# The order of the steps in an attention and mixer kernel, written anew by a search: loads, constants and the first pairs in another sequence

## The chip, the cores and the metric

The kernel runs on 1 core of one Trainium2 chip. The metric is the device time of one execution in microseconds. Of the kernel before there are three runs: 692.95 us is their median, 691.92 and 696.07 the ends.

The engines are named as the profile has them: PE is TensorE (matmuls; PEld its weight loads), DVE VectorE, ACT ScalarE, POOL GpSimd, and SP is SyncE, which issues every transfer here.

## What is computed

An attention over 4 batches, 8 heads, 576 positions and 64 values per head, then two mixers over all positions. Its core, cut:

```python
# attention: q, k, v are (4, 8, 576, 64); factor 4
q_d, k_d, v_d = mean of 4 neighbours along the sequence       # 144 positions
out_up = repeat(softmax(scale * q_d @ k_d.T) @ v_d, 4)        # pooled part
scores = where(abs(i - j) < 4, scale * q @ k.T, -1e6)         # local part
attn = out_up + softmax(scores) @ v

# first mixer, x is (4, 576, 512)
h = relu(x.T @ w_tok1) @ w_tok2;  u = x + h.T
x = u + relu(u @ w_ch1) @ w_ch2

# second mixer
theta = x @ w_theta
y = w_tok_r @ (x * cos(theta)) + w_tok_i @ (x * sin(theta))
u = x + y;  out = u + relu(u @ w_ch)
```

The weights arrive as 64-bit floats; the kernel turns them into pairs of 32-bit parts (high and low) itself, and the products of the mixers are three matmuls each (high by high, high by low, low by high).

## The kernel before

The attention is worked in pairs: pair n is two heads of one batch (16 pairs), and two pairs are a quad Q (8 quads). Every part of the program is a Python generator that issues some instructions and yields; a step is one advance of one generator. The steps have letters:

- I: the constants. First advance: the transfer `fixed<-consts` (L288); second: memsets on POOL (L290, L292); third: ACT's cast of the identity `id16` (L294).
- P: loads the queries and keys of a pair, `qk_b_p` (L324, 582 KB, four buffers). W: loads the values of the local part, `vw` (L333, four transfers). V: loads the values of the pooled part, `vd` (L342), and sums them on POOL (L344, L347, L350).
- K: pools the queries and keys of a pair on DVE (L367, L368, out `qkd`).
- F: the pooled attention of a quad: scores `sd` on PE (L380, L389), their maximum `mxd` on DVE (L398, L406), the exponential `pd` on ACT (L409, L414, L419), its transposition `pdt` on PE (L423, L428), a copy `pts` on ACT (L431, L432), the product `od` on PE (L439 to L446), the division `ods` on DVE (L450 to L453), a store of it to memory (L456, L457) and later a read back, repeated, as `xu` (L462, L465).
- L: the local attention of a pair: warm matmuls on zeros that nobody reads (L279; 24, 12, 12 and 12 for the first four pairs), the mask's matmul (L476), scores `s` (L479), `mx` and `pbuf` on DVE (L491, L492), the exponential on ACT (L499), `pt` on PE (L504), copies on ACT (L507, L508), the product `o` (L514), the division into `x` on DVE (L523 to L528).
- A adds `xu` to `x` (L541). T, E and U are the first mixer's token products (`t`, L136 to L138 and L563, L564; hidden L586, L589; out L599, L602).
- G and X convert weights: a transfer `raw` (L162), two ACT instructions (L172, L173), three on DVE (L175, L177, L185), one on POOL (L189), one on ACT (L191), the low part on DVE (L193). G0 to G6 are the token weights, X the channel weights and those of the second mixer.
- C, H, O: the first part of the channel product, from `uh` and `ul`, the split of `ut` (L627); B, M, N its second part, whose last weights are `c22` to `c25` (L645, L646, L648). R and Z switch memory over and load the second mixer's input.

The scores `s`, `sd`, the transpositions `pdt`, `pt` and the product `o` share one pool of PSUM with two buffers, taken in turn in the order of the program. `qk` has four buffers, `vw` two. All transfers are issued by SP in the order of the steps; one that must wait for its buffer holds up those behind it.

The steps stand in a table, `ORDER` (L30 to L69), a string of 1110 names: `F0` advances the pooled attention of quad 0 by one step, `L0*2` the local attention of pair 0 by two. The kernel runs through it, and within an engine the instructions stay in the order in which they are issued:

```python
    with tc.manual_schedule(engines={act.engine, dve.engine, pool.engine, pe.engine, nc.sync.engine}):
        for e in ORDER:
            name, _, times = e.partition("*")
            for _ in range(int(times or 1)):
                next(gens[name], None)
```

Behind the table comes the rest of the second mixer (z, y, out), the same code in both kernels.

Of the kernel before, what the change touches and what calls it, by code (L numbers as in the profile page):

```python
# [35 lines left out]
X0 U0.0 F3 L4 U0.0 V4 K9 F2 F3 X0 L6 L4 L6 T1 F4 U0.1 X0 F3 T1 L5 U0.1 X0 T1 U0.1 F4 X7 X4 V4 F3 T1 X7 F4 W6 L5 X7
E1.1 F4 E1.0 E1.1 L8 V4 L8 X7 E1.0 X1 A4 F4 T1 P10 A5 T1 X2 T2 L8 T1 U1.0*2 T2 T1 U1.0 X1 F3 L7 X7 L7 T2 X1 T2 X4 X5
K10 X1 L8 L6 U1.1*2 L7 T2 E2.0 U1.1 W7 X4 L7 V4 X1 L7 F4 W9 L7 L6 X4 E2.1 E2.0 C0 E2.1 T2 X1 L8 K11 X5 L7 T2 X5 L8
W8 L9*2 L7 X5 P13 T2 P12 L9 L10 C0 A6 F5 X4 C0 U2.0 L10 U2.0 X5 U2.0 C0 X3 F5 X6 F4 F5 C0 A7 F4 L10 T3 X4 F5 L9 V5
T3 H0.1 L8 U2.1 F5 T2 H0.1 H0.0 K12 T3 L9 U2.1 X5 C0 L9 U2.1 K13 F4 X6*2 L10 T3 X3 W13 H0.0 X6 H0.2 F6 E3.0*2 V5 P14  # L40
T3 F6 V5 H0.2 F6 C0 V6 V5 L8 X3 E3.1 L9 H0.3 F5 E3.1 X3 W10 L9 F6 X3 F5 L10 V6 A9 T3 F5 T3 V6 U3.0 L10 K14 T3 V6
U3.0 X6 U3.0 T3 H0.3 X3 X6 L11*2 C0 L11 P15 U3.1*2 A8 F6 U3.1 C0 F5 T4 L11 L12 L10 O0.1 K15 C0 C1 W11 L10 O0.0 C0
T4*2 F7 O0.3 O0.2 L12 C1 O0.3 T4 L12 F7 L12 T4 C1 L11 E4.1 F6 L11 F7 L11 F6 C1 A10 W12 E4.0 L11 F6 F7 E4.0 A11 F7
L12 E4.1 C1 H1.0 T5 C2 F6 L13*2 H1.1 L12 H1.1 T4 T5 T4 U4.0 L13 C1 U4.0 H1.0 U4.0 L13 V7 T4 H1.2 T5 L13 L15 L13 T4
U4.1 L12 U4.1 L15 L12 W15 V7 C1 H1.2 A12 V7 U4.1 T5 H1.3 V7 H1.3 L13 E5.0 C1 L13 F7 C1 F7 E5.0 F7 L15 L14*2 A13 L15
C1 O1.0 L14 F7 O1.1 L14 T5 W14 C1 E5.1 C2 E5.1 T6 L14 L15 L14 T5 T6 T5 U5.0 C2 T5 U5.0 L15 U5.0 T5 O1.2 T6 O1.3*2
L15 L14 T6 U5.1 L14 U5.1*2 L15 T6 E6.0 A14 A15 C2 E6.1 C3 E6.0 T7 E6.1 T6 T7 H2.0 T6 U6.0 H2.0 T7*2 U6.0*2 C3 T6*2
T7 U6.1*2 E7.0 U6.1 C2 E7.1*2 E7.0 T7 H2.1*2 T7 U7.0 T7 U7.0*2 T7 C2*2 H2.2 U7.1 H2.2 U7.1 C3 U7.1 R0 X8 X17 H2.3
X11 H2.3 C2 X19 C2*2 X8 O2.1 X8 C2 O2.2 X8 O2.0 X11 C3 O2.3*2 X21 C3 H3.0 X19 H3.0 X19 X8 C3 X17 X8 X17 C4 H3.1 C3
H3.2*2 X17 H3.1 X19 X20 H3.3 X21 H3.3 C3 X11 X9 C3 C4 O3.0 X21 X17 X19 C3 C4 X21 C3 O3.2 X11 X21 X13 C4 O3.3 O3.1  # L50
X21 O3.3 X12 X17 X9 C4 X9 X20 X19 C4 X9 H4.0 X13 H4.0 X20 C5 C4 X15 H4.2 H4.1 X9 H4.1 X20 H4.2 H4.3 B2 X16 H4.3 C4
X9 X13 C4 C5 X13 X20 C4 O4.1 X12 X10 C5 X13 C4 O4.2 X12 B2 C5 O4.0 X12 X11 X13 C5 O4.3 H5.0 X20 X16 O4.3 X23 B2 C5
H5.1 X10 H5.0 X10 C5 H5.2 X12 X11 X10 H5.1 B2 H5.3 X14 X10 H5.3 J0 H5.2 X16 C5 M2.4 X23 X10 X16 X23 X15 C5 X18 C5
O5.1 X23 X22 B2 O5.2 O5.0 X12 X15 X14 C5 X23 X14 X16 M2.5 B2 O5.3 X14 X16 O5.3 R1 B2 X15 X40 X23 X18 X30 M2.6 B2 X18
M2.5 X18 B2 M2.8 X22 M2.8 X35 X22 M2.7 B2 X15 X14 M2.4 X22 M2.6 M2.9 X18 M2.7 B2 X15 X22 X33 X14 X40 X18 X40 X30 B0
X22 M2.10 X40 M2.11 M2.9 M2.11 M2.10 B2 X40 X36 X30 X35 B2 X35 X30 B0 X33 B0 X35 X24 B2 X33 X35 X38 X30 X40 X33 B0
X30 X28 B0 X38*2 X36 B0 X36 X38 X33 B2 X35 M0.4 X36 X39 X28 M0.4 X28 X29 X38 B0 X38 X28 B0 M0.7 X27 M0.5 X36 M0.5
M0.6 M0.7 X28 X36 B0 X39 M0.6 X39 M0.8 B0 X29 X33 X39 X28 M0.9 B0 M0.10 X27 M0.8 M0.9 M0.10 M0.11 B1 X27 X24 X37
X39*2 M0.11 B0 X24 B0 X24 B1 X27 X34 B1 X27 X25 B0 X24 N0.0 X27 X29 X34 N0.0 X29 B0 X34 X25 X31 X24 B1 N0.3*2 X25
N0.3 B1 M1.4 N0.1 X25 M1.4 N0.2 B1 X34 N0.3 M1.5 X37*2 B1 N0.2 X37 N0.2 B1 M1.7 X25 M1.7 X37 X32 M1.5 X26 X29 N0.0  # L60
B1 M1.6 X29 M1.6 X37 N0.1 B1 M1.9 N0.1 X31 M1.9 X31 M1.8 B1 X34 X32 M1.8 X31 X25 M1.11 B5 M1.10 J1 X26 M1.10 M1.11
B1 X26 X32 X26 B1 B5 X32 X26 B5 X32 B1 N1.0 N1.1*2 N1.0 N1.1 B1 B5 N1.3 X26 N1.2 N1.3 B5 X34 N1.3*2 B5 M5.5 N1.0
M5.4 B5 M5.6*2 M5.5 N1.2 B5 M5.4 N1.2 J2 B5*2 M5.9 M5.7 X31 M5.7 M5.8 M5.9 B5 M5.8 M5.10 N2.0*2 N2.3 M5.11 B4 M5.10
M5.11 B5 N2.3 N2.1 N2.3 B5 B4*2 B5 X31 N2.1 N2.2 X32 R2 N2.3 N2.0 N2.1 B4*2 N2.2*2 B4 Z B5 M4.4 M4.5 M4.6*2 M4.4
M4.5 B4*2 M4.7 J4 B4 M4.8 B4 M4.9 ZS M4.9 M4.8 ZS B4 M4.10 M4.7 ZS M4.11 B3 M4.11 M4.10 B4*2 N4.0 B3 B4 N4.1*2 B3
# [918 lines left out]
```

## Time and profile before

| what | value |
|---|---|
| time, median of 3 runs | 692.95 us (691.92 to 696.07) |
| time of the profiled execution | 696.01 us |
| its span in the trace | 694.24 us (1.77 us lie around it) |
| PE busy | 672.2 us (97%), 7416 matmuls |
| PE's weight loads | 643.4 us (93%), beside the matmuls |
| DVE busy | 433.6 us (62%) |
| ACT, POOL busy | 293.0 us (42%), 94.8 us (14%) |
| mean granted PE clock | 0.982 of full speed |
| transfers | 100.36 MB, of which 0.95 MB are instructions in 58 packets |

Busy times are of one execution on the one core. A row of a timeline gives the start, the time from the first start to the last end of a run of like instructions, the engine, the line, the operation, what it writes from what it reads, and how many; in brackets how long the engine was idle just before, and which instruction or transfer released it. "issue" there means that the profile shows nothing that the engine waited for. A row of the table by stretches gives, for a stretch of the span, the busy time of each engine in it with the number of instructions, the granted PE clock, the transfers' share and their rate.

### The profile page before, as it was taken

How to read it: one execution, taken by the hardware profiler on the slowest of the kernel's cores; microseconds unless marked ns; L12 is line 12 of the kernel's file. 1: busy time of each engine (PE TensorE's matmuls, PEld its weight loads, DVE VectorE, ACT ScalarE, POOL GpSimd, SP SyncE). 2: the span in 40 equal slices, each digit the busy share in tenths (PEclk: the TensorE clock that was granted, in tenths of full speed). 3: DMA queues.
4: the chain of work that ended last, by engine and by line, in shares of the span. 5: the costliest groups of instructions: out<-in, count | busy, mean ns of one | idle time of the engine just before them, and what ended most of it. 6: DMA issues, size and time to landing. Idle time of an engine off the chain costs nothing.

```text
...
## 1 busy us (share of the span) xinstructions
PE 672.2 (97%) x7416; PEld 643.4 (93%) x7416; DVE 433.6 (62%) x765; ACT 293.0 (42%) x572; POOL 94.8 (14%) x79
## 2 busy tenths in 40 slices
PE   7679899999999999999999999999999999999998
...
GB/s 287 196 277 215 242 258 279 180 164 171 87 144 156 194 277 210 209 152 154 121 235 55 141 199 123 89 144 197 6 62 35 186 1 18 180 1 17 52 1 69
DMA packets 85611, 100.36 MB, mean 145 GB/s; under 512 B 44256, under 2 KB 65888, under 8 KB 85536
## 3 DMA queue, kind: packets, MB, share of 16 engines
...
q8 instruction: 58, 0.95, 0.6%
...
## 4 chain that ended last, share of the span: by engine, by line
PE 91%; DMA 3%; ACT 2%; DVE 2%; SPq 1%; issue 1%; DVEq 0%; ACTq 0%
PE c L645 7%; PE c L136 7%; PE c L137 7%; PE c L646 7%; PE c L648 7%; PE c L138 7%; PE y L137 6%; PE y L138 6%; PE y L136 6%; PE o L138 2%; PE o L136 2%; PE o L137 2%; PE th L138 2%; PE th L137 2%; PE th L136 2%; PE t L136 2%
## 5 line engine op out<-in xcount | busy, mean ns | idle before, releaser
L189 POOL TENSOR_TENSOR ww<-ww,raw 128x512 int32<-128x512 int32 (+2 forms) x43 | 63.9, 1490 | 187.8 <-DVE ww L185 85.3
L661 ACT ACTIVATE g<-c 128x384 fp32r<-128x384 f32 x72 | 34.3, 493 | 106.3 <-PE c L138 91.1
L136 PE MATMUL y<-wrh,zh 128*128 128x288 f32 x256 | 75.5, 296 | 0.0
L137 PE MATMUL y<-wrl,zh 128*128 128x288 f32 x256 | 75.4, 296 | 0.0
L138 PE MATMUL y<-wrh,zl 128*128 128x288 f32 x256 | 74.9, 295 | 0.0
L664 DVE SCALAR_TENSOR_TENSOR g<-c,g 128x384 fp32r<-128x384 f32 x72 | 37.9, 551 | 46.0 <-ACT g L661 39.6
L878 DVE TENSOR_TENSOR cx<-y,cx 128x288 f32<-128x288 f32 x32 | 14.6, 456 | 58.3 <-PE y L138 58.3
L672 DVE TENSOR_TENSOR ut<-c,ut 128x384 f32<-128x384 f32 x48 | 25.7, 549 | 36.6 <-PE c L648 28.3
L136 PEld LDWEIGHTS y<-wrh,zh 128*128 128x128 f32 x256 | 48.1, 188 | 0.0
L137 PEld LDWEIGHTS y<-wrl,zh 128*128 128x128 f32 x256 | 48.0, 188 | 0.0
L132 ACT CAST cuh<-cx 128x576 fp32r<-128x576 f32 x16 | 10.8, 674 | 88.1 <-DVE cx L878 88.1
L138 PEld LDWEIGHTS y<-wrh,zl 128*128 128x128 f32 x256 | 47.8, 188 | 0.0
L172 ACT ACTIVATE ww<-raw 128x512 f32<-128x512 f32 (+2 forms) x43 | 29.2, 679 | 24.3 <-DMA raw<-w_ch 6.9
L137 PE MATMUL o<-cul,wch 128*128 128x288 f32 x128 | 37.7, 295 | 0.0
L138 PE MATMUL o<-cuh,wcl 128*128 128x288 f32 x128 | 37.7, 295 | 0.0
L136 PE MATMUL o<-cuh,wch 128*128 128x288 f32 x128 | 37.3, 295 | 0.0
L173 ACT ACTIVATE raw<-raw 128x512 int32<-128x512 uint32 (+3 forms) x48 | 32.0, 666 | 0.0
L136 PE MATMUL th<-thh,cxh 128*128 128x512 f32 (+1 forms) x92 | 31.6, 343 | 0.0
L137 PE MATMUL th<-thl,cxh 128*128 128x512 f32 (+1 forms) x92 | 31.6, 343 | 0.0
L138 PE MATMUL th<-thh,cxl 128*128 128x512 f32 (+1 forms) x92 | 31.6, 343 | 0.0
L185 DVE SCALAR_TENSOR_TENSOR ww<-raw,ww 128x512 uint32<-128x512 uint32 (+2 forms) x43 | 30.4, 707 | 1.5
L175 DVE TENSOR_SCALAR ww<-ww 128x512 f32<-128x512 f32 (+2 forms) x43 | 23.0, 535 | 4.9 <-ACT ww L172 4.6
(242 smaller groups left out, 2041.8 us busy)
## 6 DMA issues: line engine op xcount, KB each, us to landing
...
```

The source lines that it names most:

```text
L136: pe.matmul(out, lh, rh, start=start, stop=False)
L137: pe.matmul(out, lh, rl, start=False, stop=False)
L138: pe.matmul(out, ll, rh, start=False, stop=stop)
L172: act.activation(w, high, AF.Abs)
L173: act.activation(f, words[:, :, 0], AF.Copy, scale=2.0**-29)
L185: dve.scalar_tensor_tensor(out=wu, in0=words[:, :, 1], scalar=0xC0000000, in1=wu, op0=ALU.bitwise_and, op1=ALU.bitwise_or)
L189: pool.tensor_tensor(out=w.bitcast(I32), in0=w.bitcast(I32), in1=f, op=ALU.add)
L645: pe.matmul(ps[:, 0:MIX], h[:, cb % 2, d], h1, start=cb == cbs[0], stop=False)
L646: pe.matmul(ps[:, 0:MIX], l[:, cb % 2, d], h1, start=False, stop=False)
L648: pe.matmul(ps[:, 0:MIX], weight[cb // 2][2][:, cb % 2, d], h2, start=False, stop=cb == cbs[-1])
L661: act.activation(h1, ps, AF.Relu)
L664: dve.scalar_tensor_tensor(out=h2, in0=ps, scalar=0.0, in1=h1.bitcast(F32), op0=ALU.max, op1=ALU.subtract)
```

## The change

All of `ORDER` is another string, of the same steps in another sequence; no other line differs. Its beginning:

```diff
 ORDER = """
-G3 P0 G2 I*2 P1 G3 P4 G3 V0 P2 G3 K0 G3 G2 I G2 I L0*2 P3 K1 F0 W1 L0 F0 L1 L0 G3 F0 V0 L1*2 P5 V0 L2 W0 G2 K2 V0 G2
-F0 G1 L1 V1 F0 L2 K3 G0 G6 K4 L0 F0 L0 L2 L1 G2 F1 L2 K5 L1 L0 F1 G1*2 F1 F0 V1 W3 L0 F1 G5 G0 L1 F0 G0 F1 G6 F2 L1
...
+P0 I*2 P1 G2 P2 P3 K0 I L0*2 L1 L0 P4 G6 G3 K1 L0 W0 F0 G2 L1 V0 K2 G1 G0 F0 P5 L1 F0 K3 F0 K4 G6 L0 G2 F0 G6 L0 G2
+L2 G3*2 F1 V0 L2 F1 V0 G1 L2 V1 V0 W1 G1 F0 F1 L0 G4 F0 G1 G0 F0 K5 L2 G5 L1 W2 G0 L1 V1 L1 L0 G1 F1*2 G6 L1 G3 F0
...
```

The order of the transfers on SP from the start of the program, before:

```order
L162 DMA raw_0_131<-w_tok2 128x288
L324 DMA qk_0_0_133<-qkT 128x1164
L162 DMA raw_1_135<-w_tok1 64x256 x2
L288 DMA fixed_79<-consts 128x227
L324 DMA qk_0_1_142<-qkT 128x1164
L324 DMA qk_1_0_146<-qkT 128x1164
L342 DMA vd_0_0_151<-vtok 128x1300
L324 DMA qk_0_2_153<-qkT 128x1164
L324 DMA qk_0_3_234<-qkT 128x1164
```

and in the changed kernel:

```order
L324 DMA qk_0_0_131<-qkT 128x1164
L288 DMA fixed_79<-consts 128x227
L324 DMA qk_0_1_137<-qkT 128x1164
L162 DMA raw_0_139<-w_tok1 64x256 x2
L324 DMA qk_0_2_142<-qkT 128x1164
L324 DMA qk_0_3_144<-qkT 128x1164
L324 DMA qk_1_0_236<-qkT 128x1164
L162 DMA raw_1_238<-w_tok2 128x288
L162 DMA raw_2_240<-w_tok2 128x288
L333 DMA vw_0_0_246<-vloc 32x1170 x2
L333 DMA vw_0_0_246<-vloc 6x1170 x2
L342 DMA vd_0_0_314<-vtok 128x1300
```

The queries and keys of batch 0's pairs 0 to 3 come in turn ahead of pair 4 (`qk_1_0`), the constants stand second and no weights ahead of them, and the pooled values `vd_0_0` have moved from the seventh place to the twelfth.

DVE from its third instruction on, before:

```order
L175 TENSOR_SCALAR raw_0_131<-raw_0_131 128x288
L177 TENSOR_SCALAR raw_0_131<-raw_0_131 128x288
L185 SCALAR_TENSOR_TENSOR raw_0_131<-raw_0_131 128x288
L367 TENSOR_TENSOR qa_0_0_157<-qk_0_0_133 128x576
L368 TENSOR_TENSOR qkd_0_0_156<-qa_0_0_157 128x288
L175 TENSOR_SCALAR raw_1_135<-raw_1_135 128x256
L177 TENSOR_SCALAR raw_1_135<-raw_1_135 128x256
L185 SCALAR_TENSOR_TENSOR raw_1_135<-raw_1_135 128x256
L367 TENSOR_TENSOR qa_0_1_236<-qk_0_1_142 128x576
L368 TENSOR_TENSOR qkd_0_0_156<-qa_0_1_236 128x288
L491 TENSOR_REDUCE mx_0_0_265<-s_0_0_167 128x10
L492 TENSOR_TENSOR pbuf0_113<-s_0_0_167,mx_0_0_265 128x2x5x38
```

and in the changed kernel:

```order
L367 TENSOR_TENSOR qa_0_0_147<-qk_0_0_131 128x576
L368 TENSOR_TENSOR qkd_0_0_146<-qa_0_0_147 128x288
L491 TENSOR_REDUCE mx_0_0_233<-s_0_0_151 128x10
L492 TENSOR_TENSOR pbuf0_113<-s_0_0_151,mx_0_0_233 128x2x5x38
L367 TENSOR_TENSOR qa_0_1_242<-qk_0_1_137 128x576
L368 TENSOR_TENSOR qkd_0_0_146<-qa_0_1_242 128x288
L367 TENSOR_TENSOR qa_0_2_317<-qk_0_2_142 128x576
L368 TENSOR_TENSOR qkd_0_1_316<-qa_0_2_317 128x288
L398 TENSOR_REDUCE mxd_0_0_324<-sd_0_0_251 128x4
L406 TENSOR_REDUCE mxd_0_0_324<-sd_0_0_251 64x1 x2
L491 TENSOR_REDUCE mx_0_1_330<-s_0_1_218 128x10
L492 TENSOR_TENSOR pbuf1_114<-s_0_1_218,mx_0_1_330 128x2x5x38
```

The weight conversions have left this place (three of them stand together behind the pooling of pair 4, ahead of `mxd_0_1`), and the maximum of the first local scores follows the first pooling at once.

PE behind the start of `s_0_2` (its mask matmuls, L476, stand ahead of these rows), before:

```order
L504 MATMUL pt_0_1_487<-fixed_79,pbuf1_114 128x128 x5
L380 MATMUL sd_0_1_494<-qkd_0_1_366 32x144 x8
...
L514 MATMUL o_0_0_522<-vw_0_0_360,plt_0_0_481 32x65 x40
L423 MATMUL pdt_0_1_596<-fixed_79,pd_0_1_573 128x128 x5
L428 MATMUL pdt_0_1_596<-fixed_79,pd_0_1_573 32x128 x8
L514 MATMUL o_0_1_614<-vw_0_1_260,plt_0_1_519 32x65 x40
L380 MATMUL sd_1_0_666<-qkd_1_0_442 32x144 x8
```

and in the changed kernel:

```order
L380 MATMUL sd_0_1_404<-qkd_0_1_316 32x144 x8
...
L479 MATMUL s_0_2_384<-qk_0_2_142 32x38 x40
...
L514 MATMUL o_0_0_526<-vw_0_0_246,plt_0_0_380 32x65 x40
L504 MATMUL pt_0_1_594<-fixed_79,pbuf1_114 128x128 x5
L423 MATMUL pdt_0_1_610<-fixed_79,pd_0_1_519 128x128 x5
L428 MATMUL pdt_0_1_610<-fixed_79,pd_0_1_519 32x128 x8
L514 MATMUL o_0_1_628<-vw_0_1_481,plt_0_1_601 32x65 x40
L380 MATMUL sd_1_0_674<-qkd_1_0_358 32x144 x8
```

The pooled scores of the second pair of pairs, `sd_0_1`, now stand ahead of `s_0_2`'s scores, and `pt_0_1` behind `o_0_0`. On DVE `x_0_0` and `x_0_1` now follow each other at once, with `mxd_1_0` behind them; before, a weight conversion stood between the two.

## Rows read from the trace of the kernel before

**Rows 1.** The page: busy time of each engine, and PE in 40 equal slices.

```profile
PE 672.2 (97%) x7416; PEld 643.4 (93%) x7416; DVE 433.6 (62%) x765; ACT 293.0 (42%) x572; POOL 94.8 (14%) x79
PE   7679899999999999999999999999999999999998
```

**Rows 2.** The table by stretches; columns as in the first line.

```profile
core 0: us, PE busy (x) PEld busy (x) DVE busy (x) ACT busy (x) POOL busy (x), PEclk, DMA share, GB/s
0.00:8.28 8.28, 4.75 (x24) 2.83 (x25) 2.85 (x8) 3.49 (x7) 2.57 (x8) 1.00 0.79 257
8.28:21.81 13.53, 9.20 (x327) 6.75 (x328) 9.69 (x18) 4.45 (x12) 3.46 (x4) 0.97 0.94 303
21.81:35.00 13.19, 10.49 (x271) 8.09 (x276) 9.80 (x20) 7.05 (x18) 1.82 (x1) 0.63 0.50 168
35.00:50.00 15.00, 10.95 (x406) 8.28 (x391) 12.42 (x25) 9.39 (x24) 4.80 (x6) 0.84 0.89 280
50.00:64.42 14.42, 13.58 (x324) 11.56 (x324) 12.73 (x26) 7.98 (x18) 7.33 (x8) 0.82 0.75 222
64.42:106.30 41.88, 38.57 (x1125) 33.57 (x1123) 39.66 (x71) 28.64 (x65) 12.06 (x10) 0.96 0.78 247
...
220.00:295.00 75.00, 75.00 (x430) 75.00 (x429) 62.39 (x106) 43.00 (x75) 24.74 (x17) 1.00 0.70 233
```

**Rows 3.** DVE's timeline: start, time, line, what; idle before and its releaser.

```profile
6.09 0.76 DVE L367 TENSOR_TENSOR qa<-qk 128x576 f32<-128x576 f32 x1 [0.96 <-DMA qk<-qkT]
6.89 0.46 DVE L368 TENSOR_TENSOR qkd<-qa 128x288 f32<-128x288 f32 x1
...
15.01 0.55 DVE L491 TENSOR_REDUCE mx<-s 128x10 f32<-128x380 f32 x1 [1.49 <-PE s L479]
...
22.19 0.55 DVE L491 TENSOR_REDUCE mx<-s 128x10 f32<-128x380 f32 x1 [2.31 <-PE s L479]
...
25.09 1.47 DVE L368 TENSOR_TENSOR qkd<-qa 128x288 f32<-128x288 f32 x1
28.45 0.76 DVE L398 TENSOR_REDUCE mxd<-sd 128x4 f32<-128x576 f32 x1 [1.89 <-PE sd L389]
...
104.52 1.75 DVE L627 TENSOR_TENSOR ul<-ut,uh 128x1536 fp32r<-128x1536 f32 x1
```

**Rows 4.** PE's timeline of the first 36 us.

```profile
1.21 4.75 PE L279 MATMUL s<-zero 128*128 128x320 bf16 x24 [1.21 <-POOL zero L290]
8.28 0.34 PE L476 MATMUL s<-fixed,id 128*128 128x190 bf16 x2 [2.32 <-ACT id L294]
...
14.60 0.31 PE L479 MATMUL s<-qk 64*32 64x38 f32 x17 [0.70 <-issue]
...
17.86 0.87 PE L479 MATMUL s<-qk 64*32 64x38 f32 x76
21.81 0.34 PE L479 MATMUL s<-qk 64*32 64x38 f32 x4 [3.08 <-issue]
...
31.90 1.33 PE L423 MATMUL pdt<-fixed,pd 128*128 128x128 f32 x5 [2.70 <-ACT pd L419]
33.16 1.08 PE L428 MATMUL pdt<-fixed,pd 128*32 128x128 f32 x16
34.17 1.41 PE L514 MATMUL o<-vw,plt 38*32 38x65 f32 x80
```

**Rows 5.** Timelines of SP (the first two transfers' issues) and of POOL.

```profile
0.74 0.39 SPq L162 DMA_DIRECT2D raw<-w_tok  x1
1.19 0.42 SPq L324 DMA_DIRECT2D qk<-qkT  x1
...
24.43 1.82 POOL L344 TENSOR_TENSOR vd<-vd 128x650 f32<-128x650 f32 x1 [9.02 <-DMA vd<-vtok]
```

**Rows 6.** Timelines of DVE and PE around 293 us.

```profile
293.37 0.69 DVE L193 TENSOR_TENSOR c25l<-ww,c25h 128x512 fp32r<-128x512 f32 x1
...
295.25 0.33 PE L646 MATMUL c<-g,c25l 128*128 128x384 f32 x1
```

More of the change, by code (lines that the diff above doesn't have):

```diff
@@ L36 @@
[L36 to L65, printed above, removed]
@@ new lines @@
+X5 U1.1 L7 L6 U1.1 X1 L8 U1.1 E2.0 T2 L6 L7 V4 F3 X1 X4 L8 E2.1 L7 L8 F4 X1 L7 X4 C0 E2.0 X5 L7 E2.1 K11 T2*2 U2.0
+X5 L9*2 U2.0 L7 U2.0 X5 T2 X6 W8 L9 C0 L10 T2 A6 P12 F5 C0 U2.1 X4 L10 X5 U2.1 A7 C0 L9 U2.1 F5 P13 T3 W9 L10 F5 C0
+T3 X5 F5 H0.1 F4 T3 L9 H0.0 X4 T3 F4 L10 H0.0 X6 V5 K12 C0 E3.0 F5 K13 F4 L9 H0.1 L8 H0.2 X3 F6 L8 W10 V5 T3 X6 P14
+V5 L9 E3.1 E3.0 C0 L9 X6 H0.2 V5 X6 E3.1 T3 X3 T3 X3 U3.0 L10 U3.0 F6 X3 T3 L10 U3.0 V6 H0.3 T3 H0.3 X3*2 L11 F5 A9
+L11 X6 U3.1*2 A8 F6 C0 U3.1 P15 L11 V6 F5 L11 C0 T4 O0.0 F5 V6 W11 V6 L10 F6 L10 C1 F6 F5 C0 T4 K14 T4 L12*2 C0 O0.1
@@ new lines @@
+O0.2 L12 C1 L11 O0.3 T4 L11 K15 O0.3 L12 C1 F7 E4.0 T4 E4.0 F7*2 F6 C2 W12 C1 E4.1 L11 H1.0 F7 L11 C1 F6 E4.1 F6 A10
+T4 W14 A11 L13*2 U4.0 T5 C1 V7 L13 H1.1 F7 H1.0 H1.1 T4 T5 H1.2 L13 L12 U4.0 H1.2 T4 T5 U4.0 L12 V7 L13 L12 L13 C2
+V7 C1 W13 V7 U4.1 F6 T4 L12 T5 U4.1 L13 E5.0 H1.3*2 C1 W15 E5.0 C2 U4.1 T5 L13 F7 E5.1*2 C1 A13 A12 T6 C1 O1.1 L14*2
+O1.2 F7 C1 L14 F7 T6 L14 L15*2 L14 O1.3 F7 T5 L15 L14 T5 O1.0 U5.0 L15*2 U5.0 T5 T6 U5.0 O1.3 L15 T6 T5 E6.0 U5.1
+L15 E6.0 U5.1*2 L14 T6 L14 L15 C2 E6.1 C3 A15 E6.1 T6 A14 T7 T6 U6.0 T6 T7 U6.0 H2.0 U6.0 T6 H2.0 T7*3 E7.0 C3 E7.0
```

32 lines of the change are left out of this document (26 added, 6 removed).

## Prediction, made before the changed kernel ran

> **What bounds the kernel now.** I read the page first. TensorE is busy for 97% of the span, and the slices of its row show where the missing 3% are: of the 40 slices (17.4 us each) only the first three, the fifth and the last lie below nine tenths [rows 1]. So the kernel is bound by TensorE nearly to its end, and an order of the same steps can only win what TensorE loses ahead of that. The table by stretches puts edges on it [rows 2]. From 106.30 on TensorE is never idle (the row 220 to 295 stands for the four stretches to 650, and the tail is the same work in both kernels). Before 106.30 it is busy 87.5 of 106.3 us: 18.8 us are lost.
>
> Who makes it wait? The same table has VectorE beside it. Up to 64.42 VectorE is busy 47.5 us and idle 16.9 (5.43, 3.84, 3.39, 2.58 and 1.69 in the five stretches). From 64.42 to 106.30 it is busy 39.66 of 41.88: there VectorE is the bound, TensorE waits for it, and this ends at the split of the first mixer input, L627 at 104.52 [rows 3], from which TensorE runs without a gap. The quantity to forecast is therefore when VectorE reaches L627. In both orders 162 VectorE instructions stand ahead of it and they are the same set, so its time is the work of these, equal but for what contention adds, plus the idle time among them. Then the timeline of VectorE tells what ended each idle [rows 3]: at 6.09 it is the first query-key block (DMA), at 15.01 and 22.19 it is TensorE's local scores s (1.49 and 2.31 us), at 28.45 the pooled scores sd (1.89 us). TensorE's own timeline tells why these were late [rows 4]: s_0_0 waits at 8.28 for the identity from the constants, 2.32 us; and at 14.60 and 21.81 it waits 0.70 and 3.08 us for nothing but "issue".
>
> These two stand 256 instructions apart, each matmul counted with its weight load: between them lie the last 17 of s_0_1, 12 warm matmuls, the start of s_0_2, pdt_0_0 and 76 of the 80 of s_0_2. I read them as instruction blocks that come late: TensorE runs through a block of small matmuls in under 5 us while the next one takes longer to arrive. The boundary ahead of 14.60 falls, counted in instructions, at 9.2 (the end of s_0_0), so one block took 5.4 us and the next 7.2.
>
> **What the change does to each term.** Everything but the table of step names is equal; TensorE, VectorE and the transfers do the same work. I sum VectorE's idle time ahead of the pooled maximum mxd_1_1 (64.42 to 65.7 now).
>
> First block. qk_0_0 is now SyncE's first transfer instead of second: it was issued at 1.19 behind 147 KB of weights and landed by 6.09 [rows 3, 5]. Issued at 0.74, without those bytes ahead of it, it lands between 4.6 (the weights' share gone) and 5.6 (only the issue gained). I take 4.6. The three weight instructions (1.15 us of VectorE) that filled a part of the wait are no longer there, so idle to this point is 4.5 us against 5.0 in before up to 6.09.
>
> Identity. The constants are second instead of fifth on SyncE, and ScalarE's cast of the identity no longer stands behind two weight conversions. s_0_0 can start when the 24 warm matmuls end, 5.96 [rows 4], not at 8.28. With 1.2 us of matmuls it ends at 7.2. VectorE has finished the first pooling (0.76 + 0.46 [rows 3]) at 5.8: idle 1.4 us. If the constants are no earlier than their old time, it is 2.3 us more.
>
> Block fetch. The same 256 instructions lie behind s_0_0, so the first boundary is passed at 7.0, and the next block is there 5.4 us later, at 12.4, if it takes what it took in before. By then VectorE has in its new order mx and pbuf of s_0_0, two poolings and mxd_0_0, work until about 11.8: idle 0.6 for s_0_1. With 7.2 us it would be 2.4. Behind this VectorE has two poolings and three weight conversions in a row, 5.9 us, during which TensorE brings sd_0_1: no idle where before had 2.31 and 1.89, and mxd_0_1 starts at about 20 instead of 28.45.
>
> A new wait. In the new order o_0_1 stands behind pdt_0_1 on TensorE, and pdt_0_1 takes the score buffer that x_0_0 frees (two buffers are used in turn by s, sd, pdt, pt and o). VectorE's next instruction behind x_0_0 is x_0_1, which waits for o_0_1: pdt (1.33 and 1.08 us) and o (1.41) are 3.8 us in a row where the granted clock was 0.63 [rows 2, 4], and half of it, 1.9, were it full. I take 3.0. Behind it is mxd_1_0, so the weight conversions cannot fill this hole.
>
> The rest to mxd_1_1. From sd_1_0 on both orders hold the same steps nearly in the same places; before is idle 2.58 + 1.69 = 4.3 us there [rows 2]. The transfer of the pooled result to memory and back stands two rows earlier on SyncE, which takes half a microsecond off: 3.8.
>
> Sum: 4.5 + 1.4 + 0.6 + 3.0 + 3.8 = 13.3 us idle against 16.9, a gain of 3.6. Then contention: some VectorE instructions are stretched while GpSimd runs, as L368 with 1.47 us at 25.09 beside GpSimd's L344 (24.43, 1.82 us) against 0.46 at 6.89 [rows 3, 5]. It is one of the two longest of five such rows; by 65.7 their excess over the usual time is about 3.4 us. The new order has the same GpSimd work; if half of the meetings are missed the gain is 5.3, if none 3.6. I take **4.5 us**. The Trainium skill ("SBUF — State Buffer", Who interferes with whom) gives a reason for the stretched rows: VectorE's second port pair is shared with GpSimd as an exclusive lock, so the loser stands still. By that rule the new order may lose or win with every meeting; the trace agrees in that only instructions with two operands in SBUF are stretched.
>
> From 65.7 to L627 before has 2.2 us of VectorE idle, so the gain cannot grow much there; behind L627 TensorE is full, and a microsecond won stays won. The profiled execution took 696.01 us (span 694.24 and 1.77 around it), 3.06 above the median 692.95. The same 4.5 from each: 691.5 in the terms of that execution, **688.5 as a median**.
>
> **The rivals.**
> Contention and new waits eat it. If the excess grows by 3.4 us (each meeting twice) the gain is 0.2 to 1.1, and with s_0_1's block at 7.2 us it falls by 1.8. Speaks for it: the new order packs VectorE tighter, so GpSimd finds fewer holes. Time: about 692.
>
> The fetch is hidden. The Trainium skill ("Runtime: NRT & Kernel Launch", Instruction fetch mechanics) says that crossing a block boundary is mostly hidden, since the sequencer fetches the next block during the current one. The trace disagrees here: 0.70 and 3.08 us of issue [rows 4]. As a mechanism of this kernel: if with other steps around it the block is there in time, and the constants and qk_0_0 come as taken, the 0.6 falls away, the 3.0 shrinks to 1.9 and contention is missed altogether, 3.4 us: 3.6 + 0.6 + 1.1 + 3.4 = 8.7, so 684.3.
>
> The other side: the second pinch. At 293.37 VectorE converts the last high channel weight, c25l, done at 294.06; TensorE takes it at 295.25 [rows 6]. That is 1.2 us of slack, with VectorE busy 83% of 220 to 295 [rows 2]. TensorE arrives earlier by the gain. If the new order's conversions come later relative to the mixer's steps, each microsecond beyond the slack is paid in full: the result is slower than before once these are late by 1.2 + 4.5 = 5.7 us against TensorE. With 10 us of lateness, the time of six such conversions, it would be 697. Against it: counted over VectorE's rows, the work ahead of c25l is equal in the two orders within 1 us, and what the front wins VectorE wins too.
>
> **How the numbers follow.** A change below 1% (6.9 us) is about what a measurement of this kernel cannot tell from none. Gain of 2 to 7 us: 0.50, its own range 686 to 691. Gain of 7 or more (hidden fetch): 0.18. Gain of 2 to a loss of 2 (contention): 0.20. Slower by over 2 us (pinch, or a queue in the front that blocks): 0.12, of which 0.07 by more than 1%. Faster than 686.0 takes the hidden fetch and a little of the likeliest: 0.20; slower than 699.9: 0.07; same 0.73. The range leaves out about a tenth on each side: 684.5 to 695.0, which takes in the bounds of the first block (1.0 us), the identity (2.3), the fetch (1.8) and the contention (3.4).
>
> **What would show it.** Right: s_0_0 starts at about 6.0, mxd_0_1 at about 20, the first mixer product T0 at about 45 (52.0 now), mxd_1_1 ends near 61, L627 stands near 100, TensorE has some 14 us idle ahead of it, and none near 290. Wrong: issue waits of TensorE beyond 4 us in all, an s_0_0 that still waits for the identity, stretched VectorE rows of more than 4 us in sum before 65, or a TensorE wait for c2xl. If L627 comes 4.5 us earlier and the end doesn't, the reading that TensorE carries each microsecond to the end is wrong.

## The result, and the profile after

The changed kernel is slower: 699.30 us as the median of 17 runs (696.95 to 703.65) against 693.34 for the kernel before (17 runs on the same chip, 690.36 to 697.91). The ratio is 1.0083, with a 95% interval from 1.0064 to 1.0103: 5.96 us lost where 4.5 were forecast to be won, and outside the forecast range (684.5 to 695.0). The interval holds no 1, so the loss is more than scatter, though it is below 1%.

The profiled execution took 703.65 us, the longest of the 17, so its rows alone would mislead; more executions of both kernels follow. Its page, against [rows 1]:

```profile
PE 673.9 (96%) x7416; PEld 643.9 (92%) x7416; DVE 435.8 (62%) x765; ACT 293.1 (42%) x572; POOL 94.4 (13%) x79
...
PE   7686899999999999999999999999999999999998
```

The span is 701.8 us. PE is idle for 27.9 us instead of 22.0. The same stretches as in [rows 2]:

```profile
0.00:8.28 8.28, 7.07 (x114) 4.68 (x115) 2.07 (x5) 1.58 (x2) 1.76 (x7) 1.00 0.76 217
8.28:21.81 13.53, 9.66 (x247) 7.33 (x247) 11.34 (x23) 6.98 (x19) 2.31 (x3) 0.87 1.02 348
21.81:35.00 13.19, 6.75 (x245) 4.96 (x244) 12.30 (x20) 8.04 (x20) 8.24 (x9) 0.76 0.72 213
...
50.00:64.42 14.42, 8.92 (x170) 7.59 (x170) 9.45 (x19) 4.70 (x10) 5.82 (x5) 0.74 0.93 287
64.42:106.30 41.88, 38.40 (x983) 33.25 (x982) 34.21 (x68) 26.72 (x64) 12.71 (x10) 0.94 0.60 192
```

Up to 35 us DVE is busier than before (25.7 against 22.3 us, first three rows), but it has not done more: 46 of its instructions have started by then instead of 45, and at the usual time of their shapes (the lower quartile of that shape in the profile) they are worth 21.5 us instead of 21.3. The rest is instructions that took longer, see "Contention". From 50 on DVE is less busy than before. In the last row, where DVE was the bound with 39.66 of 41.88 us, it is busy 34.21 and idle 7.7. DVE's timeline, against [rows 3] (`x<-o` at L523 opens x_0_1; `h` at 87.88 waits behind a late mixer product):

```profile
4.40 0.76 DVE L367 TENSOR_TENSOR qa<-qk 128x576 f32<-128x576 f32 x1 [3.54 <-DMA qk<-qkT]
...
13.89 0.55 DVE L491 TENSOR_REDUCE mx<-s 128x10 f32<-128x380 f32 x1 [0.95 <-PE s L479]
...
20.33 1.33 DVE L177 TENSOR_SCALAR raw<-raw 128x288 uint32<-128x288 uint32 x1
...
22.57 0.74 DVE L398 TENSOR_REDUCE mxd<-sd 128x4 f32<-128x576 f32 x1
...
28.61 1.63 DVE L368 TENSOR_TENSOR qkd<-qa 128x288 f32<-128x288 f32 x1
...
36.08 0.17 DVE L523 TENSOR_SCALAR rl<-o 128x10 f32<-128x10 f32 x1 [1.59 <-PE o L514]
...
64.12 0.76 DVE L398 TENSOR_REDUCE mxd<-sd 128x4 f32<-128x576 f32 x1 [4.55 <-PE sd L389]
...
87.88 0.42 DVE L589 SCALAR_TENSOR_TENSOR h<-t,h 128x256 fp32r<-128x256 f32 x1 [3.22 <-ACT h L586]
...
109.34 1.76 DVE L627 TENSOR_TENSOR ul<-ut,uh 128x1536 fp32r<-128x1536 f32 x1
```

and PE's, against [rows 4]:

```profile
6.18 0.33 PE L476 MATMUL s<-fixed,id 128*128 128x190 bf16 x2
...
13.48 0.31 PE L479 MATMUL s<-qk 64*32 64x38 f32 x17 [2.41 <-issue]
...
62.88 0.73 PE L380 MATMUL sd<-qkd 64*32 64x144 f32 x13 [5.39 <-issue]
...
86.63 0.58 PE L563 MATMUL t<-xh,w1h 128*128 128x256 f32 x1 [3.38 <-issue]
...
497.76 0.41 PE L136 MATMUL y<-wrh,zh 128*128 128x288 f32 x1 [1.20 <-ACT zh L132]
```

The first rows are nearly as forecast (pooling at 4.40, s_0_0 at 6.18, mxd_0_1 at 22.57, where about 20 was forecast and before has 28.45). Then sd_1_1, which had begun at 57.1, stops after a few matmuls for 5.39 us with "issue", and TensorE stops again at 83.2, ahead of a mixer product, for 3.38. Both stand at block boundaries: counted in instructions with their weight loads, every long issue wait of both kernels falls on an instruction that is 193 more than a multiple of 256. The packets of the instruction queue show why. I take the moment at which PE enters a block as the request for the next one. The changed kernel enters a block at 53.85 and the packet of the next starts at 60.38, 6.53 us later; it enters one at 77.36 and that packet starts at 84.22. In before the same two packets start 1.2 and 1.4 us behind the entries (56.04 and 75.18). The waiting matmul starts 2.5 and 2.4 us behind its packet here, and of the 100 issue waits over 0.4 us up to 110 us, in the 20 profiles of this case, 99 end 2.2 to 2.9 us behind the start of a packet.

In the second pinch that I had feared (290 us) PE has no gap. A gap that I had not foreseen is in the last row: at 497.8 PE waits 1.20 us for zh, and ACT's cast of zh waits for a store of the first mixer's result:

```profile
497.09 0.62 ACT L132 CAST zh<-tg 128x512 fp32r<-128x512 f32 x1 [2.87 <-DMA xT<-ut]
```

### The profile page after: what moved, and what is told of

Read it like the earlier page. It is cut to its first block, busy times and chain, and to the rows that moved or that the text cites. A ratio compares the mean times of both kernels' runs of the same rounds, so it can differ in the third digit from the quotient of the medians.

```text
span 701.8 us, 17270 instructions
## 1 busy us (share of the span) xinstructions
PE 673.9 (96%) x7416; PEld 643.9 (92%) x7416; DVE 435.8 (62%) x765; ACT 293.1 (42%) x572; POOL 94.4 (13%) x79
## 4 chain that ended last, share of the span: by engine, by line
PE 87%; DVE 6%; issue 2%; DMA 2%; ACT 1%; SPq 1%; POOL 0%; DVEq 0%; ACTq 0%; POOLq 0%
PE c L136 7%; PE c L137 7%; PE c L138 7%; PE c L645 7%; PE c L648 6%; PE c L646 6%; PE y L136 5%; PE y L138 5%; PE y L137 5%; PE o L138 2%; PE o L137 2%; PE o L136 2%; PE t L136 2%; PE t L137 2%; PE t L138 2%
## 5 line engine op out<-in xcount | busy, mean ns | idle before, releaser
L189 POOL TENSOR_TENSOR ww<-ww,raw 128x512 int32<-128x512 int32 (+2 forms) x43 | 63.4, 1477 | 188.0 <-DVE ww L185 65.5
L137 PE MATMUL y<-wrl,zh 128*128 128x288 f32 x256 | 75.4, 295 | 0.0
L878 DVE TENSOR_TENSOR cx<-y,cx 128x288 f32<-128x288 f32 x32 | 14.6, 456 | 57.3 <-PE y L138 57.3
L672 DVE TENSOR_TENSOR ut<-c,ut 128x384 f32<-128x384 f32 x48 | 25.4, 549 | 25.8 <-PE c L648 16.9
L185 DVE SCALAR_TENSOR_TENSOR ww<-raw,ww 128x512 uint32<-128x512 uint32 (+2 forms) x43 | 31.9, 743 | 1.5
L177 DVE TENSOR_SCALAR ww<-ww 128x512 uint32<-128x512 uint32 (+2 forms) x43 | 26.6, 617 | 1.5
```

The costliest lines, as they stand in the source:

```text
L137: pe.matmul(out, lh, rl, start=False, stop=False)
L185: dve.scalar_tensor_tensor(out=wu, in0=words[:, :, 1], scalar=0xC0000000, in1=wu, op0=ALU.bitwise_and, op1=ALU.bitwise_or)
L189: pool.tensor_tensor(out=w.bitcast(I32), in0=w.bitcast(I32), in1=f, op=ALU.add)
```

## Experiments

### Executions of the same code

Four more executions of the two kernels, unchanged: 698.86 (e13) and 704.75 us (e15) of the changed one, 692.39 (e14) and 695.88 (e16) of before.

> The changed kernel, unchanged, profiled again. Theory (late instruction blocks as a rule): issue waits of TensorE of 7 to 12 us in sum ahead of 110 us (12.2, 9.6 and 6.2 in the three executions of this code so far, before 4.5 and, with a front of before's order, 6.1); L627 at 104 to 109; 592 to 593.5 us from L627 to the end. Rival (chance): 4 to 6 us of issue waits, L627 at 102 to 104.

> The kernel before, unchanged, profiled again. Theory: issue waits of 4 to 6.5 us in sum ahead of 110 us, L627 at 104 to 105.5, 589 to 590.5 us from there to the end. Rival (chance): issue waits anywhere from 4 to 12.

> The changed kernel, unchanged, a further execution. Theory and rival as for the thirteenth experiment; of the two executions at least one has more than 7 us of issue waits by the theory, neither by the rival.

> The kernel before, unchanged, a further execution. Theory and rival as for the fourteenth experiment; by the theory neither of the two has more than 7 us of issue waits.

Two mixed orders (below) are the changed kernel's code up to L627, so there are five executions of it up to there and three of before. Times in us; issue waits are PE's, to 110 us.

| execution | mxd_1_1 (DVE) | L627 (DVE) | from L627 to the end | issue waits |
|---|---|---|---|---|
| changed, first | 64.12 | 109.34 | 592.4 | 12.2 |
| changed, e13 | 61.19 | 105.67 | 591.3 | 6.3 |
| changed, e15 | 62.38 | 106.74 | 596.2 | 10.1 |
| e6, changed to L627 | 62.23 | 103.39 | | 6.2 |
| e11, changed to 450 us | 61.21 | 105.50 | | 9.6 |
| mean | 62.2 | 106.1 | 593.3 | 8.9 |
| before, first | 64.42 | 104.52 | 589.7 | 4.5 |
| before, e14 | 60.86 | 101.08 | 589.5 | 4.9 |
| before, e16 | 64.81 | 104.54 | 589.6 | 6.2 |
| mean | 63.4 | 103.4 | 589.6 | 5.2 |

The means add up to 6.5 us, the medians of the runs differ by 5.96: 1.1 won up to mxd_1_1, 3.9 lost from there to L627, 3.7 lost behind it. The 1.1 lies within the scatter (61.2 to 64.1 against 60.9 to 64.8) and is no gain in work: in the changed order 90 DVE instructions stand ahead of mxd_1_1, in before 94, and the four others, 1.3 us at their usual time, come behind it. The sum of both stretches is the fair comparison, since 162 stand ahead of L627 in both: 2.7 us lost.

The expected issue waits came in e15 (10.1), while e13 has 6.3, just below its range; the time from L627 to the end missed its range in both, 591.3 below it and 596.2 above. Before came as expected in its waits and its end, but e14 was faster at L627 than expected. Which block is late differs from execution to execution:

```profile
67.10 0.57 PE L479 MATMUL s<-qk 64*32 64x38 f32 x41 [2.99 <-issue]
```

is e13's longest, and e15 has these, the second and third of them behind L627:

```profile
61.14 0.72 PE L380 MATMUL sd<-qkd 64*32 64x144 f32 x13 [3.63 <-issue]
...
109.55 0.88 PE L479 MATMUL s<-qk 64*32 64x38 f32 x77 [1.95 <-issue]
...
497.35 0.61 PE L136 MATMUL y<-wrh,zh 128*128 128x288 f32 x1 [1.97 <-ACT zh L132]
```

And before has a faster front than the one I read. In e14 no issue wait stands at 14.6 and 21.8 us, and its mxd_0_1 is 5 us earlier than in [rows 3]:

```profile
23.46 0.76 DVE L398 TENSOR_REDUCE mxd<-sd 128x4 f32<-128x576 f32 x1 [0.67 <-PE sd L389]
```

### Mixed orders: which part loses

Since both tables hold the same steps, any front of the one can be followed by what is left, in the order of the other:

```python
def mixed(first, n, rest): ...   # first[:n], then the steps of rest not yet done
e1  = mixed(changed, 150, before)    # changed order to sd_1_1, about 57 us
e2  = mixed(before, 157, changed)    # before's order to pair 8's load
e6  = mixed(changed, 314, before)    # changed order to L627
e7  = mixed(e2, 314, before)         # before, changed from 57 us to L627, before
e11 = mixed(changed, 1082, before)   # changed order to the first B3, about 450 us
```

> The changed order up to the pooled scores sd_1_1 (its first 150 steps, some 57 us), then the steps that are left in the order of before. Theory (late instruction blocks): the front of the changed order is worth 3.6 us at sd_1_1 (57.09 against 60.70), and what is lost is lost behind it, where TensorE waits 5.39 and 3.38 us for instruction blocks beside the transfers of the pairs 8 and 9 and of the channel weights. These transfers stand later in before's order, so the two long issue waits go: 689 to 691, 2 to 4 us below before. Rival (the new front itself costs, by a backlog of work that it leaves for later): 697 to 700, near the changed kernel.

> The other half: before's order up to its first step of pair 8 (157 steps), then the steps that are left in the changed order. Theory (late instruction blocks): without the front's gain, and with the changed order's transfers behind it, at least one issue wait of 3 us or more between 55 and 90 us: 695 to 700. Rival (the front costs): about before's 693.

> The changed order up to the split of the first mixer input (L627), then the rest in before's order. It takes away what the changed order does behind it: in its profile TensorE is idle there 0.82 us at 159.6 (issue) and 1.20 us at 497.8 (zh, which waits for a store of the first mixer's result), where before has neither. Theory (the loss of 5.9 us is 4 in the front, 2 behind): 1.5 to 2.5 us below the changed kernel, 697 to 698, and no wait at 497. Rival (all of the loss is in the front): 699 or more.

> Before's order up to pair 8's load, the changed order from there to the split of the first mixer input, then before's order again: the second experiment without the changed order's tail. Theory: the wait at about 490 us (1.24 us in the second experiment's profile) and the 0.56 at 152 go, 692 to 694.5, 1 to 2 us below the second experiment and 0 to 2 us below before. Rival (the tail costs nothing, profiles of single executions scatter by that much): 695 to 697 as the second experiment.

> The changed order up to the first step of the last third of the channel product (B3, some 450 us), then before's order. It takes away the changed order's last stores only, behind which zh waits (1.20 us at 497.8 in the changed kernel's profile). Theory (the changed order's rest behind L627 costs 2.8 us by the medians, most of it at the end): 696.5 to 698.5, 1 to 2.5 us below the changed kernel, no wait of zh near 497. Rival (it is lost between 110 and 450 us): within 0.7 us of the changed kernel, 699.

| kernel | front | middle | end | ratio to before on its chip | 95% interval |
|---|---|---|---|---|---|
| e1 | changed | before | before | 1.0035 | 1.0010 to 1.0059 |
| e2 | before | changed | changed | 1.0014 | 0.9993 to 1.0035 |
| e6 | changed | changed | before | 1.0032 | 1.0012 to 1.0053 |
| e7 | before | changed | before | 0.9985 | 0.9965 to 1.0005 |
| e11 | changed | changed | before from 450 us | 1.0057 | 1.0027 to 1.0087 |
| changed | changed | changed | changed | 1.0083 | 1.0064 to 1.0103 |

Read in pairs: the changed front costs 0.35% (e1 against before), 0.47% (e6 against e7) and 0.69% (changed against e2), that is 2.4 to 4.8 us. The changed end costs 0.51% (changed against e6) and 0.29% (e2 against e7), 2.0 to 3.5 us, about half of it behind 450 us (e11). The middle costs nothing (-0.03 and -0.15%). The three differences for the front and the 0.51% for the end are clear of scatter; the 0.29% for the end and e11's share of it are not. My expectation for e1, 2 to 4 us faster than before, was wrong: the front itself costs, even where before's order follows. That of e2 (a wait of 3 us or more at 55 to 90 us) was wrong too; its longest there is 0.48. e6 gained more over the changed kernel than expected (0.51%, 3.5 us, instead of 1.5 to 2.5), e11 what was expected (0.26%, 1.8 us). e7 came 1.2 us below before on its chip (694.89 against 696.06), as expected, though above the range written down (692 to 694.5); its interval holds 1, so it is not shown to be faster.

In the profiles with the changed end PE waits for zh at 490 to 500 us in all (changed 1.20, 1.13 and 1.97, e2 1.24; e3, e5 and e8, below, 0.9 to 2.6), in e6, e7, e11 and the three of before in none. (e9 and e10, below, have before's end and wait for it too, 1.32 and 0.93, so the order of the end is not the only thing that brings it.) In the changed kernel this wait is 1 to 2 of the end's 2 to 3.5 us; issue waits of 0.8 to 0.9 us at 158 to 160 are in two of three changed executions as well.

### Are the blocks late because of the transfers?

> Before's order with three additional transfers of 582 KB (from the queries' and keys' memory to memory that nobody reads), issued behind the load of pair 11 at about 67.4 us, where before has no issue wait. Theory (late instruction blocks): the block requested at 70.8 us comes 3 to 7 us later than in before (0.8 us from request to its packet there), and TensorE shows an issue wait of 1 to 5 us at about 75; the time rises by 1 to 5 us. Rival (blocks don't depend on the transfers): no issue wait; waits for transfers (DMA) alone may appear.

```diff
 # before's order, behind the load of pair 11
+    def extra():
+        for i in range(3):
+            sp.dma_start(extra_d[i], qkT[3, i])
+        yield
```

The packet of the block asked for at 69.4 us started 4.25 us later (0.78 in the first execution of before), and PE has a wait that this execution of before has not. Lines of this kernel stand one lower:

```profile
76.16 0.48 PE L381 MATMUL sd<-qkd 64*32 64x144 f32 x16 [1.99 <-issue]
```

The time is 698.35 us (10 runs), ratio 1.0030 (1.0000 to 1.0061): 2.1 us, with an interval from none to 4.2, beside a wait of 1.99. One profile does not show that the transfers did it: before, unchanged, has the same wait in e14, where the packet came 3.18 us behind the entry (0.74 in e16):

```profile
73.57 0.48 PE L380 MATMUL sd<-qkd 64*32 64x144 f32 x16 [1.52 <-issue]
```

What speaks for the transfers is all 20 profiles together. Over their block boundaries up to 80 us the packet starts 1.05 us (median of 56) behind the entry where the transfers' share in the microsecond behind it is below 0.4, and 3.13 us (median of 64) where it is 1.0 or more. That they go together is shown, that the transfers are the cause is likely but not shown; nor is it shown that such a wait is paid in full. The other way round, three loads held back in the changed order:

> The changed order with three load steps moved: the queries and keys of the pairs 8 and 9 and the channel weight between them (582 + 512 + 582 KB) are issued behind the store of the pooled result od_1_0, at about 66 instead of 55.7 to 57.2 us. Theory (late instruction blocks): the block that TensorE waits for at 57.5 lies behind less data; pooled values and four value transfers (997 KB) still precede it, so the wait falls from 5.4 to 3 us or less, and the time by 1 to 4 us to 695 to 698. Rival (the block is late for another reason, for instance since TensorE runs through its block in 3.4 us): the wait stays at 5 us and the time at 699 or above, as the loads come later.

```diff
-P8 E0.1 X2 L3 X7 P9 G5 A3 X0 L5 E0.1 F2 G3 ... F2 L4 L6 F2 T0 L4 V3
+E0.1 X2 L3 G5 A3 X0 L5 E0.1 F2 G3 ... F2 L4 L6 F2 P8 X7 P9 T0 L4 V3
```

The wait got shorter, as the theory says (the packet 3.70 us behind the entry instead of 6.53), but the five executions of the changed order have 0.5 to 6.5 us at this boundary without any edit:

```profile
60.10 0.72 PE L380 MATMUL sd<-qkd 64*32 64x144 f32 x13 [2.71 <-issue]
```

The time got longer: 704.45 us, ratio 1.0116 (1.0087 to 1.0145). PE waits for the pooled queries of pair 8 now (1.7 us at 77.2, [<-DVE qkd]), and its clock is granted at half from 79.1 to 89.3, so the loads probably came too late for their own use.

### Does the place of a boundary matter?

> The changed order with 22 more warm matmuls (matmuls on zeros that nobody reads) ahead of the local scores of pair 4, at about 46.5 us. They shift every later block boundary by 44 instructions, so that the block missed at 57.5 us is asked for at the start of the first mixer products (about 50 to 51 us), ahead of the transfers issued from 53.7 on, and not 22 matmuls into them. No transfer and no step is moved. They cost 1.6 us of TensorE at full clock, 3.3 at half. Theory (a block's delay depends on which transfers are issued around its request): the 5.4 us wait goes or falls below 2, and so does the one of 3.4 at 83 us, whose block is then asked for ahead of the 582 and 2 x 512 KB at 77.6; 694 to 698, that is 1 to 5 us below the changed kernel. Rival (a boundary there is missed wherever it lies, since the work between is too short for any fetch): an issue wait of 3 us or more stays within 50 to 65 us, and the time is 699 to 703.

```diff
-WARM = [24] + [12] * 3 + [0] * 12
+WARM = [24] + [12] * 3 + [22] + [0] * 11
```

```profile
56.89 0.39 PE L137 MATMUL t<-xl,w1h 128*128 128x256 f32 x1 [2.45 <-issue]
...
65.13 0.49 PE L380 MATMUL sd<-qkd 64*32 64x144 f32 x8 [1.07 <-issue]
```

The wait split in two, and 702.67 us came out, ratio 1.0095 (1.0069 to 1.0121), against 1.0083: no gain. The wait moved with the boundary, as the theory says; the time is the one that the rival named.

> The kernel before with 6 instead of 12 warm matmuls ahead of s_0_2: 12 instructions fewer, so that the boundary that cuts off 4 of s_0_2's 80 matmuls falls behind them. Nothing else changes. Theory (late instruction blocks set the front): s_0_2 is complete at about 19 instead of 22.1 us in all executions, mxd_0_1 at 24 to 25.5 instead of 28.5, L627 at 101 to 103; 691.5 to 693.5 where before has 694 to 695, 0.2 to 0.4% faster, if no later boundary falls worse by 12 instructions. Rival (VectorE's work and order set it, or fewer warm matmuls cost clock): within 0.1% of before or slower.

```diff
-WARM = [24] + [12] * 3 + [0] * 12
+WARM = [24, 12, 6, 12] + [0] * 12
```

```profile
17.04 0.91 PE L479 MATMUL s<-qk 64*32 64x38 f32 x80
18.25 0.30 PE L504 MATMUL pt<-fixed,pbuf 128*128 128x128 f32 x1 [0.29 <-issue]
21.85 1.01 PE L504 MATMUL pt<-fixed,pbuf 128*128 128x128 f32 x4 [3.31 <-issue]
```

All 80 matmuls of s_0_2 are in time, as meant; the same wait, 3.31 us, now stands in pt_0_0, and mxd_0_1 moved from 28.45 to 26.98 only. The kernel is slower, 698.73 us, ratio 1.0047 (1.0020 to 1.0074): PE has issue waits elsewhere (1.31 us at 75.4, 2.27 us at 107.2) where the first profile of before has none, though e14 has one of 1.52 at 73.6, so whether the 12 moved instructions brought them is open.

> The same 6 warm matmuls fewer in the order of the seventh experiment (before's front and end, the changed order's middle; 0.15% faster than before there, with an interval from 0.35% faster to none). Theory: both gains add, 0.3 to 0.6% faster than before, 690.5 to 692.5. Rival: the later boundaries, moved by 12 instructions, undo one of them: 693 to 696.

The same edit in e7's order: 695.81 us, ratio 1.0012 (0.9985 to 1.0039), so neither expected gain came (690.5 to 692.5 was the theory's range), and that of e7 was not clear of scatter to begin with.

### Contention

> The changed order with GpSimd's addition (L189) left out in the seven conversions of the token weights, so the weights' low bits are not those of the input; all else stays. It is to measure the disputed term, VectorE's instructions stretched beside GpSimd: in the changed kernel their excess over the usual time adds up to 6.2 us by 57 us, against 3.4 to 3.8 in before. Theory (GpSimd is what stretches them): the excess falls by 2.5 us or more, most of it between 18 and 33 us, and the first mixer product T0 starts by 2 us earlier, at about 47.5. Rival (they are stretched by the transfers into SBUF at that time): the excess stays within 1 us of 6.2.

```diff
+            if at >= 7:
-            pool.tensor_tensor(out=w.bitcast(I32), in0=w.bitcast(I32), in1=f, op=ALU.add)
+                pool.tensor_tensor(out=w.bitcast(I32), in0=w.bitcast(I32), in1=f, op=ALU.add)
```

(Lines behind the edit stand one lower.) DVE's excess over the usual times up to 57 us fell from 6.2 to 4.6 us, less than the 2.5 expected and more than the rival's 1; T0 came at 49.01 instead of 49.41. Five executions of the changed order's front have 5.9 to 6.6 us, the three of before 2.2 to 4.3, so this front stretches DVE's rows by some 3 us more. What is left in e8 stands beside the pooled values' additions, which stayed, as this one in the changed kernel stands beside DVE's row at 28.61:

```profile
28.60 1.34 POOL L344 TENSOR_TENSOR vd<-vd 128x650 f32<-128x650 f32 x1 [0.64 <-DMA vd<-vtok]
```

The time is 698.05 us, ratio 1.0028 (0.9994 to 1.0061), against the changed kernel's 1.0083 (1.0064 to 1.0103). With GpSimd's additions left out the changed order thus loses 0.55%, 3.8 us, less. How much of that is DVE's stretched rows and how much the shorter chain of each conversion is not shown, since before was not run without these additions.

### The clock

Over the executions the mean granted clock of the changed kernel is 0.9835, that of before 0.987 (in the runs beside the experiments). The kernels with the changed front all lie low (e1 0.9834, e6 0.9816, e11 0.9828), those with before's front do not (e2 0.9877, e7 0.9869). Against before on the same chip (0.987 is taken for the changed kernel) they are 0.0035 to 0.0054 lower; of 697 us that is 2.4 to 3.8 us by my estimate, the size of the front's cost. Does the clock cost the front, or do its waits lower the clock?

> The sixth experiment (changed order up to L627, then before's order) with the 12 warm matmuls of pair 3, which stand ahead of its local scores at about 37 us, moved into the hole in which TensorE waits for x_0_0 (31 to 34.5 us), as matmuls into a spare tile that nobody reads. The number of instructions is the same, so the block boundaries behind 40 us stay. Theory (the changed front loses by TensorE's granted clock what it wins in waits: over the executions the sixth has 2.0 us less besides the clock and 3.8 more by it than before): with the hole filled the half clock of 10.2 us from about 29 to 39 us gets shorter; mean granted clock from 0.9816 to 0.984 or more, 695 to 697. Rival (the clock there is low for another reason, or the fill only delays): clock within 0.001 of 0.9816, 698 or more.

> The sixth experiment with 24 additional warm matmuls in the two holes of the front: 12 behind o_0_0 (about 26.3 to 28, where TensorE waits for ACT's exponential), 12 behind pdt_0_1 (32 to 34.5); pair 3 keeps its own. The block boundaries behind move by 48 instructions. Theory (clock): mean granted clock 0.985 or more; 694 to 697 if the moved boundaries cost nothing. Rival (boundaries moved by about as much as in the fifth experiment cost 2 to 4 us there, so here too): clock up, yet 698 to 701.

```diff
+    def fill():
+        for k, n in enumerate(FILL):
+            t = mmp.tile([128, 512], F32, tag="mm", name=f"fill_{k}")
+            warm(t[:, 0:320], n)
+            yield
-... G1 F1*2 G6 L1 ...
+... G1 F1 w F1 G6 L1 ...
```

(e9, with `WARM = [24] + [12] * 2 + [0] * 13` and `FILL = [12]`; e10 keeps `WARM` and has a second `w` behind o_0_0.) The clock rose as expected, to 0.9849 and 0.9883. The time did not fall: 698.21 us, ratio 1.0058 (1.0030 to 1.0086), and 701.04, 1.0090 (1.0057 to 1.0123), against e6's 1.0032. A higher clock bought with matmuls did not make the kernel faster, so the clock as the cause is not shown; it is not excluded either, since e9 gained only part of the difference and e10 added matmuls and moved boundaries.

### One part of the change alone

> Before's order with one part of the change alone: the queries and keys of pair 0 first, the constants second, pair 1 third, and pair 0's pooling, the cast of the identity and s_0_0 ahead of the weight conversions; all else in before's order. Theory of the prediction (a microsecond won in the front is carried to the end): pooling at 4.4 instead of 6.1, s_0_0 at 6.1 instead of 8.3, 1 to 2 us faster than before, 691.5 to 694. Theory (late instruction blocks): the first block boundary is passed 2.2 us earlier, but the block asked for there comes no earlier, being behind the same transfers, so s_0_1 still stands at 13.5 to 14.5 and the gain is 0 to 0.7: within 0.1% of before.

```diff
-G3 P0 G2 I*2 P1 G3 P4 G3 V0 P2 G3 K0 G3 G2 I G2 I L0*2 P3 ...
+P0 I*2 P1 G3 G2 P4 K0 I L0*2 G3*2 V0 P2 G3*2 G2*2 P3 ...
```

Neither theory: 702.36 us, ratio 1.0112 (1.0074 to 1.0149). The pooling came at 4.84 and s_0_0 at 6.57, as meant. But the weights, now third on SP, land later, and the conversions still stand ahead of K1 on DVE:

```profile
9.99 0.31 DVE L175 TENSOR_SCALAR raw<-raw 128x288 f32<-128x288 f32 x1 [3.90 <-ACT raw L172]
```

```profile
16.79 0.73 PE L380 MATMUL sd<-qkd 64*32 64x144 f32 x16 [8.53 <-DVE qkd L368]
```

mxd_0_0 is at 18.04 instead of 11.10, 6.9 us late, L627 is 6.0 us later than the mean of before (109.43 against 103.4), and the median is 7.6 us longer: most of what is lost in the front arrives at the end.

## Why the prediction was wrong

**What bounds the kernel: right in the main.** What is lost ahead of L627 arrives at the end (e12: 6.0 us at L627, 7.6 in the median), and from L627 to the end before takes 589.5 to 589.7 us in its three executions.

**First block, identity: right.** 4.40 and 6.18 against 4.6 and 5.96.

**Block fetch: the mechanism right, its reach missed.** The first fetch took 6.5 us (7.03 to 13.48) instead of 5.4. The Trainium skill ("Runtime: NRT & Kernel Launch", Instruction fetch mechanics) calls the crossing mostly hidden; by that rule PE would not have waited 5.39 us at one boundary, so the measurement decides. But I priced one boundary, and priced all later ones as in before, by leaving them out. Every boundary meets another set of transfers in another order; issue waits up to 110 us came to 8.9 us on average instead of 5.2.

**The sum to mxd_1_1: 1.1 us instead of 4.5.** x_0_1 waited 1.59 us, not 3.0. DVE's idle time ahead of mxd_1_1 was forecast as 13.3 us; the five executions have 13.3 to 16.5, mean 14.6. The 16.9 from which I subtracted is what two executions of before have; e14 has 14.9, and the mean is 16.2. So idle time fell by 1.6 instead of 3.6, and busy time, from which I expected 0.9 less, rose by 0.5 although four instructions fewer stand there: I summed up to a place at which the two orders have not done the same work.

**Contention: the term with the wrong sign.** I took 0.9 us won, between half of the meetings missed (1.7) and none. DVE's excess over the usual times ahead of mxd_1_1 is 5.9 to 6.6 us in the five executions and 3.0 to 5.0 in before: 2.1 us lost on average. And the sentence that only instructions with two operands in SBUF are stretched was wrong: L177 with one operand took 1.33 us at 20.33 beside GpSimd, 0.31 otherwise, and the first trace of before had such a row already, while GpSimd's L344 ran from 49.90 to 51.25:

```profile
50.09 1.32 DVE L177 TENSOR_SCALAR ww<-ww 128x288 uint32<-128x288 uint32 x1
```

The same page of the Trainium skill ("SBUF — State Buffer", Who interferes with whom) names `tensor_scalar` among the operations that can take the shared ports, and by that the trace agrees.

**The step that failed most in the front is "from 65.7 to L627".** I argued that DVE, with 2.2 us idle there, bounds it, so that a gain could only shrink a little. In the changed order DVE idles 3.5 to 7.8 us there (mean 5.7, before 2.7) and works 0.9 us longer, with the four postponed instructions: 3.9 us in all. The longest of these idle times end with ACT's h in the first execution (3.22, behind the late mixer product), with PE's s in e13 and e15 (2.1 and 2.9 in sum). A stretch bounded by DVE in one order need not be so in another.

**The other is "behind L627 a microsecond won stays won".** The order was changed behind L627 as well, and I had looked at one place only, the conversions near 293 us, which were harmless. 3.7 us went elsewhere in the three profiles, 2.0 to 3.5 by the mixed orders: zh behind the last store (1.1 to 2.0), issue waits, half clock.

The rival on the other side had the right kind of mechanism, a pinch behind the front, at the wrong place; that of contention and new waits was the nearest, but its time was about 692, since it had no loss behind mxd_1_1.

Not settled: how the front's cost of 2.4 to 4.8 us divides. L627 comes 2.7 us later on average, of which 1.4 is DVE taking longer for the same 162 instructions and 1.3 is more idle time. In the profile of e1, where before's order follows, mxd_1_1 stands at 65.30, the excess ahead of it is 6.1 us as in the changed kernel, DVE waits 1.05 and 1.99 us for ACT's w2h behind 57 us, and issue waits up to 110 us are only 4.0, no more than in before. So late blocks, which do stop PE and are more in the changed order, are not the whole of it; contention and the clock remain beside them, and each edit that moved a boundary (e5, e10, e17) or a load (e3, e12) brought losses of its own.
